# Two rounds of linear attention and feed-forward on one core: the attention's denominators spread by DMA instead of by matmuls, its sum over the rows cut in two halves, and the layer norms rearranged

## The chip, the cores and the metric

One core of a Trainium2 chip runs the whole program. The metric is the time of one execution in microseconds (us) of the device; the median of the runs shown is compared. A profiled execution, taken separately, gives the trace that every reading here comes from. Engines are named as the profile names them: PE (matrix multiply, with PEld for its weight loads), ACT (scalar engine), DVE (vector engine), POOL (GpSimd) and SP (the queue that issues DMAs).

## The reference

Two kinds of layer, each run twice on 2048 rows of 512 features (bf16), the second pair with the same weights as the first:

```
def _A_ref(x, wqkv, wo):                      # x: layer-normed rows
    H = 32; Dh = 16
    q, k, v = split(x @ wqkv)                 # 32 heads of 16
    phi = lambda t: where(t > 0, t + 1, exp(t)) + 1e-6
    pq, pk = phi(q), phi(k)
    kv  = einsum("bhsd,bhse->bhde", pk, v)    # sum over all rows
    z   = einsum("bhsd->bhd", pk)
    num = einsum("bhqd,bhde->bhqe", pq, kv)
    den = einsum("bhqd,bhd->bhq", pq, z)[..., None] + 1e-6
    return (num / den).reshape(B, S, D) @ wo

def _B_ref(x, w1, w2):                        # 512 -> 1376 -> 512
    return max(x @ w1, 0) @ w2

x = x + _A_ref(layernorm(x), wqkv, wo);  x = x + _B_ref(layernorm(x), w1, w2)
x = x + _A_ref(layernorm(x), wqkv, wo);  x = x + _B_ref(layernorm(x), w1, w2)
```

There is no mask and no position, so any order of the rows gives the same result as long as loads and stores agree.

## The kernel before

The 2048 rows are 16 tiles of 128 rows, and four tiles make a chunk (chunks 0 to 3). Layers 0 and 2 are attention, called A0 and A2 here; layers 1 and 3 are feed-forward, B1 and B3. All weights and activations stay in SBUF. `xn` holds the normed rows, `Tb` their transposes (features on partitions), `xres` the residual in f32.

An attention layer goes through these steps. `a_k` computes K of one tile (4 matmuls of 512 columns), `a_q` Q of one chunk, transposed (16 matmuls). `phi_evac` turns each into phi with two passes of ACT (lines 493 and 495) and two of DVE (497 and 503), into units of the buffer `big`. `a_z` sums phi(K) over the rows by matmuls of one column. `a_g` computes xn^T pk into four banks of PSUM (64 matmuls of 512 columns), from which `a_kv` makes K^T V by multiplying with the V weights, so that V itself is never computed. `a_m` masks the heads and multiplies by `wo`, giving `Mf` in four parts. `a_den` computes the denominators of a chunk, one row per head in a 32-row layout, and ACT takes their reciprocals as exp(-ln) into `rdc`. `a_pqs` spreads each reciprocal over the 16 rows of its head with four matmuls against the 0/1 matrix `Esel` (the group `rdc,Esel` of the profile) and multiplies phi(Q) by the result on DVE, out of PSUM (line 606). `a_fin` multiplies phi(Q) by `Mf` (16 matmuls per chunk), and `resid` adds it to the residual (DVE, line 521) and takes the sum of squares (ACT, line 527).

A feed-forward layer computes `h` per chunk in eleven parts, ten of 128 columns by `b_h` (40 matmuls) and one of 96 (`b_h_rest`, 16 matmuls of 96 columns, and a DMA transpose, line 642), and then `b_out`, eleven matmuls per tile.

Between two layers `ln_chunk` computes mean and variance of a chunk from the two sums in four small DVE steps (lines 439 to 445), a power of -1/2 on POOL (line 447) and one more DVE step (449). `ln_norm` then normalizes each tile on ACT, DVE or POOL. The transposes of a chunk go to the DMA (`transpose_chunk`, line 467) or, for the first chunk after an attention layer (`A_PE_CHUNKS=1`) and the first two chunks of the program (`FIRST_PE_CHUNKS=2`), to PE (`transpose_pe`, line 481) with an evacuation on ACT or DVE.

The order of instructions on each engine is fixed before the program runs. The code records every operation with its engine, what it reads and writes, and a planned duration, and `_list_schedule` goes through the records, giving PSUM banks (eight) and a place in an engine's order to whatever could start first within a window. Some operations may go to ACT or DVE, whichever would end first. Layers are interleaved: the steps of the next layer that need only finished chunks are put between the steps of this one. On the chip each engine then works through its list in order, waiting on semaphores; SP does the same with the DMAs. A step that waits therefore holds up everything behind it on its engine.

At the start `ld_x` loads x, in the order tile 0, the rest of chunk 0, K weights, Q weights, the other chunks, V weights, `wo`, `w1`, `w2`. Row 128n+p goes to partition p of tile n. The first DMA transpose waits for all loads (`ALL_LOADS`). While nothing has arrived, 16 matmuls on zeros run (`WARM`, line 399).

Of the kernel before, what the change touches and what calls it, by code (L numbers as in the profile page):

```python
# [16 lines left out]
C_MM128 = 58.0  # L17
C_MM96 = 43.0
# [14 lines left out]
C_POOL_POW = 1000.0  # L33
C_POOL_NORM = 900.0
C_SP_ISSUE = 60.0
TAIL = {PE: 70.0, ACT: 230.0, DVE: 80.0, POOL: 300.0, SP: 0.0}
# [208 lines left out]
def build_kernel(nc, A_x, A_wqkv, A_wo, B_w1, B_w2, out, n_layers_pairs=2, K_STT=0, Q_STT=0, A_PE_CHUNKS=1, windows=None,  # L245
                 WARM=16, SPLIT0=True, TAIL_SPLIT=True, LAST_HALVES=True, FIRST_PE_CHUNKS=2,
# [16 lines left out]
    UNITS = max(8, NFC) * NCH  # L263

    es = contextlib.ExitStack()
    with es:
# [14 lines left out]
        NL = 2  # L281
        lnd = sb("lnd", [128, NL, 512], F32)
        rdc = sb("rdc", [128, NCH, 512], BF16)
        hm128 = sb("hm128", [128, 4, 32], BF16)
        hm1 = sb("hm1", [128, 4, 32], F32)
        Esel = sb("Esel", [128, 128], BF16)
# [20 lines left out]
        veps0 = sb("veps0", [128, 1], F32)  # L307
        rstd0 = sb("rstd0", [128, 1], F32)
        nbias0 = sb("nbias0", [128, 1], F32)
# [28 lines left out]
        def dma(emit, reads, writes, xfer_ns, name):  # L338
            sem = es.enter_context(nc.semaphore("dsem%d" % len(dma_sems)))
            dma_sems.append(sem)  # L340

            def _emit(eng, emit=emit, sem=sem):
                return emit(eng).then_inc(sem, 16)
            op = g.add(SP, _emit, reads, writes, dur=C_SP_ISSUE, lat=xfer_ns, dma=True, name=name)
            op.seq = sem
            return op
# [17 lines left out]
        x_v = A_x[0].rearrange("(n p) d -> p n d", p=128)  # L364
        out_v = out[0].rearrange("(n p) d -> p n d", p=128)
        def ld_x(t, lo=0):
            dma(lambda e, t=t: e.dma_start(xin[:, 4 * t + lo:4 * t + 4, :], x_v[:, 4 * t + lo:4 * t + 4, :]),
                [], [("xin", i) for i in range(4 * t + lo, 4 * t + 4)], 1500.0 * (4 - lo) / 4.0, "ld_x%d" % t)
        dma(lambda e: e.dma_start(xin[:, 0, :], x_v[:, 0, :]), [], [("xin", 0)], 450.0, "ld_x0a")
        wq_v = A_wqkv.rearrange("(c p) n -> p c n", p=128)  # L370
        ld_x(0, 1)
        dma(lambda e: e.dma_start(wqkv[:, :, D:2 * D], wq_v[:, :, D:2 * D]), [], [("wk",)], 1500.0, "ld_wk")  # L372
        dma(lambda e: e.dma_start(wqkv[:, :, 0:D], wq_v[:, :, 0:D]), [], [("wq",)], 1500.0, "ld_wq")  # L373
        for t in range(1, NCH):
# [5 lines left out]
        dma(lambda e: e.dma_start(w1[:], B_w1.rearrange("(c p) n -> p c n", p=128)), [], [("w1",)], 4000.0, "ld_w1")  # L380
        dma(lambda e: e.dma_start(w2[:, 0:nfull, :], B_w2[0:nfull * 128, :].rearrange("(c p) n -> p c n", p=128)),
            [], [("w2a",)], 3800.0, "ld_w2a")
        if FLAST < 128:
            dma(lambda e: e.dma_start(w2[0:FLAST, NFC - 1, :], B_w2[nfull * 128:DFF, :]), [], [("w2b",)], 600.0, "ld_w2b")
        W2KEYS = [("w2a",), ("w2b",)] if FLAST < 128 else [("w2a",)]
        ALL_LOADS = [("wk",), ("wv",), ("wq",), ("wo",), ("w1",)] + W2KEYS
# [6 lines left out]
        if WARM > 0:  # L393
            wt = alloc_bank()

            def _warm(e):
                last = None
                for k in range(WARM):
                    last = e.matmul(psv[:, wt, :], wrm[:, 0:128], wrm[:, :], start=True, stop=True)
                return last  # L400
            g.add(PE, _warm, [("wrm",)], [("ps", wt)], WARM * 400.0, name="warm")
# [12 lines left out]
        ones_v = onesf[:, :].rearrange("p (j r) -> p j r", r=32)  # L414
        g.add(POOL, lambda e: e.affine_select(hm1[:], ones_v, [[0, 4], [-16, 32]], ALU.is_ge, 0.0, base=0, channel_multiplier=1),
              [("onesf",)], [("hm1",)], 350, name="as_h1")
        g.add(POOL, lambda e: e.affine_select(hm128[:], hm1[:], [[0, 4], [16, 32]], ALU.is_ge, 0.0, base=15, channel_multiplier=-1),
              [("hm1",)], [("hm128",)], 350, name="as_h2")

        def head_rows():  # L420
            b = alloc_bank()
            g.add(PE, lambda e: e.transpose(psv[:, b, 0:64].bitcast(BF16), hm128[:].rearrange("p j r -> p (j r)"), ident[:]),
                  [("hm128",), ("ident",)], [("ps", b)], C_MM128, name="trh")
            g.add(DVE, lambda e: e.tensor_copy(Esel[:], psv[:, b, 0:64].bitcast(BF16)), [("ps", b)], [("Esel",)], 200.0, name="esel")

        def ln_stats_first(i):
            g.add(DVE, lambda e: e.bn_stats(bst[:, i, :], xin[:, i, :]), [("xin", i)], [("bst", i)], C_DVE_BNST, name="bnst%d" % i)  # L427
            g.add(DVE, lambda e: e.bn_aggr(mv[:, i, :], bst[:, i, :]), [("bst", i)], [("mean", i), ("var", i)], C_DVE_SMALL, name="bnag%d" % i)

        def ln_chunk(t, first):  # L430
# [6 lines left out]
            else:  # L437
                mean_ap = mean[:, sl]
                g.add(DVE, lambda e: e.tensor_scalar(mean[:, sl], s1[:, sl], INV_D, None, ALU.mult),
                      [("s1", i) for i in tl], [("mean", i) for i in tl], C_DVE_SMALL, name="mean%d" % t)  # L440
                g.add(DVE, lambda e: e.scalar_tensor_tensor(nm2[:, sl], mean[:, sl], -1.0, mean[:, sl], ALU.mult, ALU.mult),
                      [("mean", i) for i in tl], [("nm2", t)], C_DVE_SMALL, name="nm2_%d" % t)
                g.add(DVE, lambda e: e.scalar_tensor_tensor(var[:, sl], s2[:, sl], INV_D, nm2[:, sl], ALU.mult, ALU.add),
                      [("s2", i) for i in tl] + [("nm2", t)], [("var", i) for i in tl], C_DVE_SMALL, name="var%d" % t)
                g.add(DVE, lambda e: e.tensor_scalar(veps[:, sl], var[:, sl], 0.0, EPS, ALU.max, ALU.add),  # L445
                      [("var", i) for i in tl], [("veps", t)], C_DVE_SMALL, name="veps%d" % t)
            g.add(POOL, lambda e: e.tensor_tensor(rstd[:, sl], veps[:, sl], nhalf[:, 0:4], ALU.pow),  # L447
                  [("veps", t), ("nhalf",)], [("rstd", t)], C_POOL_POW, name="rstd%d" % t)
            g.add(DVE, lambda e: e.scalar_tensor_tensor(nbias[:, sl], mean_ap, -1.0, rstd[:, sl], ALU.mult, ALU.mult),
                  [("mean", i) for i in tl] + [("rstd", t)], [("nbias", t)], C_DVE_SMALL, name="nbias%d" % t)  # L450

        def ln_norm(i, first):
            t = i // 4
            src = xin[:, i, :] if first else xres[:, i, :]
            skey = ("xin", i) if first else ("xres", i)
            rd = [skey, ("rstd", t), ("nbias", t)]
            alts = [(ACT, lambda e: e.activation(xn[:, i, :], src, ACTF.Identity, scale=rstd[:, i:i + 1], bias=nbias[:, i:i + 1]),
                     C_ACT_SB_AP),
                    (DVE, lambda e: e.tensor_scalar(xn[:, i, :], src, rstd[:, i:i + 1], nbias[:, i:i + 1], ALU.mult, ALU.add),  # L459
                     C_DVE_NORM_BF if first else 460.0)]  # L460
            if not first:
                alts.append((POOL, lambda e: e.tensor_scalar(xn[:, i, :], src, rstd[:, i:i + 1], nbias[:, i:i + 1], ALU.mult, ALU.add),
                             C_POOL_NORM))
            g.add_flex(alts, rd, [("xn", i)], name="norm%d" % i)

        def transpose_chunk(t, extra_reads=()):
            dma(lambda e: e.dma_start_transpose(Tb[:, 4 * t:4 * t + 4, :, :].rearrange("p i c t -> p (i c) t"),
                                                xn[:, 4 * t:4 * t + 4, :].rearrange("p i d -> p (i d)")),
                [("xn", i) for i in range(4 * t, 4 * t + 4)] + list(extra_reads),
                [("T", i) for i in range(4 * t, 4 * t + 4)], 2950.0, "tr%d" % t)  # L470
# [72 lines left out]
        def a_zc(ZB):  # L543
            g.add(DVE, lambda e: e.tensor_tensor(Zc[:], hm128[:], psv[:, ZB, 0:4].unsqueeze(2).broadcast_to([128, 4, 32]), ALU.mult),
                  [("ps", ZB), ("hm128",)], [("Zc",)], 200.0, name="zc")

        def a_g(m, i0, GB):
            def mk():
                mms = []
                for i in range(i0, i0 + 4):  # L550
                    u = pk_unit(i)
                    mms.append((psv[:, GB, :], xn[:, i, 128 * m:128 * m + 128], big[:, u * 512:u * 512 + 512],
                                i == 0, i == NT - 1, True))
                return mms
            mm_group(mk, [("xn", i) for i in range(i0, i0 + 4)] + [("big", pk_unit(i)) for i in range(i0, i0 + 4)],
                     [("ps", GB)], 4 * C_MM512, "g%d_%d" % (m, i0 // 4))

        def a_g_evac(m, GB):
            g.add_flex([(ACT, lambda e: e.activation(GT[:, m, :], psv[:, GB, :], ACTF.Identity), C_ACT_PSUM),
                        (DVE, lambda e: e.tensor_copy(GT[:, m, :], psv[:, GB, :]), C_DVE_FLEX)],  # L560
                       [("ps", GB)], [("GT", m)], name="gev%d" % m)

        def a_kv(m, KB):
# [410 lines left out]
```

## Time and profile before

| | us |
|---|---|
| median of 3 runs (293.8 to 294.86) | 294.8 |
| the profiled execution, as a run | 295.03 |
| its span in the trace | 293.3 |
| PE busy | 283.8 |
| ACT busy | 170.3 |
| DVE busy | 158.1 |
| POOL busy | 33.1 |

The span is measured from the first to the last instruction of the trace, so 1.7 us of the profiled run lie outside it. PE's ends are modelled, and a PE that is called busy may be waiting inside a group of matmuls; what a matmul really takes is read from the starts of one group after another. Sixteen matmuls of 512 columns take 3.45 us in this way (from 32.83 to 36.28 us of the trace), 0.216 us each, and the granted clock is 1.00 throughout.

### The profile page before, as it was taken

Reading aid. Unit: us, or ns where it says so; the run is one execution under the profiler, and the core shown is the slowest. Engines: PE = TensorE matmul, PEld = TensorE weight load, DVE = VectorE, ACT = ScalarE, POOL = GpSimd, SP = SyncE. Lnnn points to the kernel's source line nnn. Section 1 sums busy time; section 2 is a strip of 40 time slices with the busy share of each in tenths; the row PEclk is TensorE's granted clock in tenths of the full one; section 3 lists DMA queues with packets and bytes.
Section 4 is the critical chain, followed back from the end, with each engine's and each line's share of the span. In section 5 each row is a group of like instructions: output and inputs, shape, how many; then the busy total and the mean of one; then the engine's idle time right before and its main releaser. Section 6 shows DMA issues by size and latency. Waiting matters only on the chain.

```text
span 293.3 us, 4232 instructions
## 1 busy us (share of the span) xinstructions
PE 283.8 (97%) x1610; PEld 133.5 (46%) x1636; DVE 158.1 (54%) x443; ACT 170.3 (58%) x351; POOL 33.1 (11%) x43
## 2 busy tenths in 40 slices
PE   7699999989999999999999999999999999999996
PEld 3345444434454454454444444444445445454444
DVE  5699774999720293361454748928973037020122
ACT  2798496687765365397434999248786505407000
POOL 4012100002410040020020300000241002000000
PEclk9999999999999999999999999999999999999999
DMA  7991330000260016031003300000026003303022
GB/s 221 356 370 41 64 54 0 2 0 0 52 130 0 2 35 126 1 71 21 0 2 72 70 4 0 0 2 0 1 58 124 0 2 91 72 2 89 0 74 72
DMA packets 37796, 16.72 MB, mean 57 GB/s; under 512 B 29616, under 2 KB 37264, under 8 KB 37776
## 3 DMA queue, kind: packets, MB, share of 16 engines
q1 hardware_dynamic: 37776, 16.45, 22.8%
q8 instruction: 13, 0.21, 0.3%
q14 instruction: 7, 0.06, 0.1%
HBM read 7.01 MB, written 2.10 MB: 31 GB/s over the span
## 4 chain that ended last, share of the span: by engine, by line
PE 88%; DVE 6%; DMA 3%; ACT 2%; issue 1%; SPq 1%
PE ps L510 87%; DMA xin<-in_A_x_dram 3%; DVE big L606 2%; DVE xn L459 1%; DVE xres L521 1%; ACT Mf L576 1%; ACT big L493 1%; PE ps L481 0%; DVE bst L427 0%; DVE big L503 0%; DVE emscr L497 0%; ACT sqscr L527 0%; SPq L373 0%; ACT escr L495 0%; SPq L372 0%
## 5 line engine op out<-in xcount | busy, mean ns | idle before, releaser
L510 PE MATMUL ps<-w,big 128*128 128x512 bf16 (+3 forms) x355 | 76.0, 372 | 0.4
L510 PE MATMUL ps<-Tb,w 128*128 128x512 bf16 x320 | 70.4, 379 | 0.0
L510 PEld LDWEIGHTS ps<-w,big 128*128 128x128 bf16 (+1 forms) x363 | 35.3, 98 | 40.4
L527 ACT ACTIVATE sqscr<-xres 128x512 bf16<-128x512 f32 x48 | 30.0, 628 | 40.1 <-DVE xres L521 39.6
L655 ACT ACTIVATE big<-ps 128x512 bf16<-128x512 f32 x70 | 41.6, 598 | 17.9 <-PE ps L510 17.9
L510 PEld LDWEIGHTS ps<-Tb,w 128*128 128x128 bf16 x320 | 30.8, 98 | 35.9
L493 ACT ACTIVATE big<-ps 128x512 bf16<-128x512 f32 x64 | 41.2, 648 | 9.0 <-PE ps L510 8.8
L521 DVE SCALAR_TENSOR_TENSOR xres<-ps,xres 128x512 f32<-128x512 f32 x32 | 21.9, 689 | 38.2 <-PE ps L510 38.0
L495 ACT ACTIVATE escr<-ps 128x512 bf16<-128x512 f32 x64 | 41.6, 667 | 0.4 <-DVE emscr L497 0.4
L447 POOL TENSOR_TENSOR rstd<-veps,nhalf 128x4 f32<-128x4 f32 x15 | 16.1, 1070 | 204.5 <-DVE veps L445 183.3
L518 DVE TENSOR_TENSOR xin<-ps,xres 128x512 bf16<-128x512 f32 x15 | 10.4, 692 | 46.6 <-PE ps L510 46.6
L510 PE MATMUL ps<-wqkv,Tb 128*128 128x512 bf16 x122 | 28.6, 379 | 2.7 <-DVE Tb L486 1.2
L510 PE MATMUL ps<-Tb,wqkv 128*128 128x512 bf16 x128 | 30.6, 379 | 0.0
L510 PE MATMUL ps<-Mf,big 128*128 128x512 bf16 x122 | 29.0, 380 | 1.3 <-ACT Mf L576 0.8
L510 PE MATMUL ps<-big,xn 128*128 128x512 bf16 x124 | 29.7, 379 | 0.3
L497 DVE TENSOR_SCALAR emscr<-escr 128x512 bf16<-128x512 bf16 x64 | 18.4, 296 | 18.5 <-ACT escr L495 18.4
L503 DVE TENSOR_TENSOR big<-big,emscr 128x512 bf16<-128x512 bf16 x64 | 26.4, 421 | 1.2
L606 DVE TENSOR_TENSOR big<-big,ps 128x512 bf16<-128x512 bf16 x32 | 19.9, 680 | 1.3 <-PE ps L510 1.3
L510 PEld LDWEIGHTS ps<-wqkv,Tb 128*128 128x128 bf16 x128 | 12.1, 98 | 17.2 <-DVE Tb L486 1.7
L510 PEld LDWEIGHTS ps<-Mf,big 128*128 128x128 bf16 x128 | 11.9, 98 | 16.2 <-ACT Mf L576 1.3
L510 PEld LDWEIGHTS ps<-big,xn 128*128 128x128 bf16 x128 | 11.5, 97 | 13.1 <-issue 1.5
L510 PEld LDWEIGHTS ps<-Tb,wqkv 128*128 128x128 bf16 x128 | 11.5, 97 | 12.3 <-DVE big L606 0.4
(74 smaller groups left out, 196.2 us busy)
## 6 DMA issues: line engine op xcount, KB each, us to landing
wqkv<-in_A_wqkv_dram SPq DMA_DIRECT2D x3, 512.0 KB, 7.1
xin<-in_A_x_dram SPq DMA_DIRECT2D x3, 512.0 KB, 9.1
out_dram<-xin SPq DMA_DIRECT2D x3, 512.0 KB, 2.9
w<-in_B_w_dram SPq DMA_DIRECT2D x1, 1376.0 KB, 11.0
w<-in_B_w_dram SPq DMA_DIRECT2D x1, 1280.0 KB, 12.8
wo<-in_A_wo_dram SPq DMA_DIRECT2D x1, 512.0 KB, 9.4
xin<-in_A_x_dram SPq DMA_DIRECT2D x1, 384.0 KB, 3.2
out_dram<-xin SPq DMA_DIRECT2D x1, 256.0 KB, 2.1
```

The lines of the kernel that those rows point to most:

```text
L447: g.add(POOL, lambda e: e.tensor_tensor(rstd[:, sl], veps[:, sl], nhalf[:, 0:4], ALU.pow), [("veps", t), ("nhalf",)], [("rstd", t)], C_POO ...
L459: (DVE, lambda e: e.tensor_scalar(xn[:, i, :], src, rstd[:, i:i + 1], nbias[:, i:i + 1], ALU.mult, ALU.add), C_DVE_NORM_BF if first else 4 ...
L493: g.add(ACT, lambda e: e.activation(dst_ap, psv[:, b, :], ACTF.Identity, bias=1.0 + 1e-6, scale=1.0), [("ps", b)], [dst_key], C_ACT_PSUM, ...
L495: g.add(ACT, lambda e: e.activation(escr[:, s, :], psv[:, b, :], ACTF.Exp), [("ps", b)], [("escr", s)], C_ACT_EXP, name=name + "_exp")
L497: g.add(DVE, lambda e: e.tensor_scalar(emscr[:, s, :], escr[:, s, :], 1.0, 1e-6, ALU.min, ALU.add), [("escr", s)], [("emscr", s)], C_DVE_B ...
L503: g.add(DVE, lambda e: e.tensor_tensor(dst_ap, dst_ap, emscr[:, s, :], ALU.max), [dst_key, ("emscr", s)], [dst_key], 340.0, name=name + "_ ...
L510: last = e.matmul(o, l, r, start=st, stop=sp, skip_group_check=skip)
L518: g.add(DVE, lambda e: e.tensor_tensor(xin[:, i, :], psv[:, b, :], src, ALU.add), [("ps", b), skey], [("xin", i)], C_DVE_PSUM, name="resid ...
L521: g.add(DVE, lambda e: e.scalar_tensor_tensor(xres[:, i, :], psv[:, b, :], 0.0, src, ALU.add, ALU.add, accum_out=s1[:, i:i + 1]), [("ps", ...
L527: g.add(ACT, lambda e: e.activation(sqscr[:, q, :], xres[:, i, :], ACTF.Square, accum_out=s2[:, i:i + 1]), [("xres", i)], [("sqscr", q), ( ...
L606: g.add(DVE, lambda e, j=j, u=u: e.tensor_tensor(unit_ap(u), unit_ap(u), psv[:, bs[j], :], ALU.mult), [("ps", bs[j]), ("big", u)], [("big" ...
L655: g.add_flex([(ACT, lambda e, M=M, b=b, u=u: e.activation(unit_ap(u, M), psv[0:M, b, :], ACTF.Relu), C_ACT_PSUM), (DVE, lambda e, M=M, b=b ...
```

## The change

- Denominators. `a_pqs` has no matmuls any more. The reciprocals `rdc` are copied by four DMAs from SBUF to SBUF (`a_spread`), each source row to four partitions, into units of `big`, and DVE multiplies two SBUF tiles. For this each row of `a_den`'s result now stands for a head four times (`hm32` in place of `hm128` and `Esel`). Chunk 0 is spread by itself, chunks 1 and 2 together, chunk 3 by itself.
- xn^T pk. `a_g` works on 256 of the 512 columns. The first half is computed chunk by chunk while K and Q are, in both attention layers; the second half in `bar`. `a_kv`, `a_m` and the evacuations are done per half. `a_fin` of the first six tiles is split into j = 0, 1 and j = 2, 3, so that the first part needs only the first half.
- Norms between layers. The small steps of `ln_chunk` move from DVE to POOL, five of them before the power and one behind it. DVE and POOL normalize with (x + (-mean)) * rstd; each tile of a chunk has a fixed engine (two DVE, one ACT, one POOL).
- Transposes. `A_PE_CHUNKS` is 0: the first chunk after an attention layer is transposed by two DMAs of two tiles. The first DMA transpose no longer waits for `w1` and `w2`; these are loaded after the transposes of chunks 2 and 3 have landed.
- Start. Tiles 0 to 3 have a chain each (`ln_own`): statistics, power, normalization, PE transposes. Tile 3's statistics are taken on ACT. Partition p holds rows 16p to 16p+15, so a load or store of several tiles is contiguous for each partition. 13 warming matmuls.
- The planner's durations are adjusted (for example POOL's tail of 300 ns becomes 60, the issue of a DMA transpose 1200), which shifts the order on every engine.

```
-    A_PE_CHUNKS=1, WARM=16
+    A_PE_CHUNKS=0, WARM=13
+        FIN_SPLIT = 6
-        x_v = A_x[0].rearrange("(n p) d -> p n d", p=128)
+        x_v = A_x[0].rearrange("(p n) d -> p n d", p=128)
+        def ld_ff():
+            after = [("T", i) for i in range(4 * FIRST_PE_CHUNKS, NT)]
+            dma(..., after, [("w1",)], 4000.0, "ld_w1")
...
-        ALL_LOADS = [("wk",), ("wv",), ("wq",), ("wo",), ("w1",)] + W2KEYS
+        ALL_LOADS = [("wk",), ("wv",), ("wq",), ("wo",)]
...
         def ln_chunk(t, first):
-                g.add(DVE, lambda e: e.tensor_scalar(mean[:, sl], s1[:, sl], INV_D, None, ALU.mult), ...
-                g.add(DVE, lambda e: e.scalar_tensor_tensor(nm2[:, sl], mean[:, sl], -1.0, mean[:, sl], ALU.mult, ALU.mult), ...
-                g.add(DVE, lambda e: e.scalar_tensor_tensor(var[:, sl], s2[:, sl], INV_D, nm2[:, sl], ALU.mult, ALU.add), ...
-                g.add(DVE, lambda e: e.tensor_scalar(veps[:, sl], var[:, sl], 0.0, EPS, ALU.max, ALU.add), ...
+                g.add(POOL, lambda e: e.tensor_scalar(mean[:, sl], s1[:, sl], -INV_D, None, ALU.mult), ...
+                g.add(POOL, lambda e: e.tensor_tensor(nm2[:, sl], s1[:, sl], mean[:, sl], ALU.mult), ...
+                g.add(POOL, lambda e: e.tensor_scalar(nm2[:, sl], nm2[:, sl], D * EPS, None, ALU.add), ...
+                g.add(POOL, lambda e: e.tensor_tensor(var[:, sl], s2[:, sl], nm2[:, sl], ALU.add), ...
+                g.add(POOL, lambda e: e.tensor_scalar(veps[:, sl], var[:, sl], INV_D, EPS, ALU.mult, ALU.max), ...
             g.add(POOL, lambda e: e.tensor_tensor(rstd[:, sl], veps[:, sl], nhalf[:, 0:4], ALU.pow), ...
...
+        def a_g(m, i0, n, hf, GB, col, opens):
...
+                    mms.append((psv[:, GB, col:col + 256], xn[:, i, 128 * m:128 * m + 128],
+                                big[:, u * 512 + 256 * hf:u * 512 + 256 * hf + 256], opens and i == 0, i == NT - 1, True))
...
+        def a_spread(t0, n):
+            w = 512 * n
+            for j in range(4):
+                u = rb_unit(t0, j)
+                dma(lambda e, j=j, u=u: e.dma_start(big[:, u * 512:u * 512 + w],
+                                                    rdc[32 * j:32 * j + 32, t0:t0 + n, :].rearrange("p t q -> p (t q)")
+                                                    .unsqueeze(1).broadcast_to([32, 4, w])), ...
         def a_pqs(t):
-            bs = [alloc_bank() for _ in range(4)]
-            mm_group(lambda: [(psv[:, bs[j], :], Esel[32 * j:32 * j + 32, :], rdc[32 * j:32 * j + 32, t, :], ...
             for j in range(4):
-                g.add(DVE, lambda e, j=j, u=u: e.tensor_tensor(unit_ap(u), unit_ap(u), psv[:, bs[j], :], ALU.mult), ...
+                u, r = pq_unit(j, t), rb_unit(t, j)
+                g.add(DVE, lambda e, u=u, r=r: e.tensor_tensor(unit_ap(u), unit_ap(u), unit_ap(r), ALU.mult), ...
...
+        def a_fin_chunk(t, first_layer):
+            if t == 0:
+                for i in range(FIN_SPLIT):
+                    fin_open[i] = alloc_bank()
+                    a_fin_mm(i, fin_open[i], (0, 1))
...
+        def ln_own(i):
+            g.add(POOL, lambda e: e.tensor_tensor(rstd[:, i:i + 1], veps[:, i:i + 1], nhalf[:, 0:1], ALU.pow), ...
+            g.add(DVE, lambda e: e.tensor_scalar(xn[:, i, :], xin[:, i, :], mu, rstd[:, i:i + 1], ALU.subtract, ALU.mult), ...
+            transpose_pe(i)
...
                 def bar():
+                    g_a(NCH - 1)
...
+                    a_den(NCH - 1)
+                    a_spread(NCH - 1, 1)
...
                 def p2(t):
-                    for i in range(4 * t, 4 * t + 4):
-                        a_fin(i, first_layer)
-                    ln_next(t, t < A_PE_CHUNKS)
+                    a_fin_chunk(t, first_layer)
...
+                    ln_next(t, t < A_PE_CHUNKS, 2 if t == 0 else 1)
```

In the order that the planner makes of this, all 64 matmuls of `a_fin` of a layer now stand together (before, twelve of them stood behind the first feed-forward chunks), and DVE's list holds the multiplications by spread reciprocals between other steps: in A0 the phi of Q's last tile behind the second DMA of chunk 0, and the first residual of chunk 0 behind the first DMA of chunk 3; in A2 the second half's head mask behind the third DMA of chunk 3.

## The prediction

> **What bounds the kernel now.** I read the page's busy times and chain of waits first, then PE's instructions in order of time, then the ends of the waits in the first 35 us and between A0 and B1.
>
> ```profile
> PE 283.8 (97%) x1610; PEld 133.5 (46%) x1636; DVE 158.1 (54%) x443; ACT 170.3 (58%) x351; POOL 33.1 (11%) x43
> PE 88%; DVE 6%; DMA 3%; ACT 2%; issue 1%; SPq 1%
> ```
>
> PE is the bound nearly everywhere, so a change pays where it takes matmuls off PE or closes one of PE's few gaps, and costs where it opens one. In PE's order of time (start, length, line, group, idle before):
>
> ```profile
> 17.01 1.36 PE L481 MATMUL ps<-ident,xn 128*128 128x128 bf16 x16
> 19.29 3.40 PE L510 MATMUL ps<-wqkv,Tb 128*128 128x512 bf16 x15
> 32.83 3.62 PE L510 MATMUL ps<-wqkv,Tb 128*128 128x512 bf16 x16
> 50.26 1.03 PE L510 MATMUL ps<-big,xn 128*128 128x512 bf16 x4
> 51.22 0.39 PE L510 MATMUL ps<-rdc,Esel 32*128 32x512 bf16 x4
> 51.55 0.40 PE L510 MATMUL ps<-GT,wqkv 128*128 128x128 bf16 x4
> ...
> 60.22 3.63 PE L510 MATMUL ps<-Mf,big 128*128 128x512 bf16 x16 [0.79 <-ACT Mf L576]
> ...
> 67.14 3.63 PE L510 MATMUL ps<-Mf,big 128*128 128x512 bf16 x15
> 70.60 1.06 PE L481 MATMUL ps<-ident,xn 128*128 128x128 bf16 x16
> 71.75 1.90 PE L510 MATMUL ps<-Mf,big 128*128 128x512 bf16 x8
> 73.49 0.84 PE L510 MATMUL ps<-w,Tb 128*128 128x96 bf16 x16
> ...
> 166.03 0.25 PE L510 MATMUL ps<-ones,big 128*128 128x1 bf16 x4 [0.41 <-DVE big L503]
> ```
>
> The reader should subtract starts, not add lengths: a length holds 0.16 us of pipeline that overlaps the next group. Four xn^T pk matmuls from 50.26 end their turn at 50.26 + 4 x 0.216 = 51.12; the next group but one starts at 51.55, so the spreading group takes 0.43.
>
> For what replaces PE's work, the DMAs to landing and POOL's power:
>
> ```profile
> Tb<-xn SPq DMA_TRANSPOSE x12, 4.3
> xin<-in_A_x_dram SPq DMA_DIRECT2D x1, 128.0 KB, 2.2
> big<-hr SPq DMA_TRANSPOSE x8, 2.4
> out_dram<-xin SPq DMA_DIRECT2D x1, 128.0 KB, 1.7
> ```
>
> ```profile
> 23.57 1.65 POOL L447 TENSOR_TENSOR rstd<-veps,nhalf 128x4 f32<-128x4 f32 x1 [7.35 <-DVE veps L435]
> 66.91 1.01 POOL L447 TENSOR_TENSOR rstd<-veps,nhalf 128x4 f32<-128x4 f32 x1 [33.82 <-DVE veps L445]
> ```
>
> **The parts, one by one.** The sum is against the profiled execution: span 293.3, run 295.03, 0.2 above the median of 294.8. What comes off the span I take off the median.
>
> *Spreading matmuls.* Eight groups (four chunks, two layers) of 0.43: **-3.4**. Their DVE multiply (line 606, eight in 4.87 us, 0.61 each out of PSUM) becomes an SBUF one like line 503 (two in 0.75 us), 32 x 0.24 = 7.7 us of DVE, worth nothing on PE by itself. In exchange twelve DMAs per layer go to SP. The trace has no SBUF-to-SBUF copy. Nearest rows of 128 KB: 1.7 and 2.2; farthest that fits a DMA inside the core, 4.3 for a transpose. I take 2.2 (same size, same kind of instruction), and 0.6 for issuing one (rows 0.40 to 0.51 on SP). SP has nothing else queued: in A0 `w1`, `w2` are issued ahead of them once chunk 3's transpose has landed (issued at 34.7 as before, plus 4.5), from about 39 to 47 (before, they landed 7.3 us after `wo`; B1 needs them at 72), and the first reciprocal is ready at about 50; the first transpose behind them is needed at 67. Walking A0 by these: chunk 0's second copy lands at 53.0, Q's last phi behind it on DVE is done at 53.7, `a_den` of chunk 3 reads it at 54.5; chunk 3's first copy lands at 60.1, the first residual behind it could start at 60.7. A2's third copy of chunk 3 lands 0.4 before the mask behind it is due. All covered, by half a microsecond each.
>
> *PE transposes between layers.* 67.14 + 16 x 0.216 = 70.60 to 71.75 is 1.15 with its 0.28 idle; twice: **-2.3**. Now the DMA path must be ready when the 64 `a_fin` matmuls end, since the 96-column group behind them needs all of chunk 0, and all of the feed-forward layer stands behind that group on PE. A0: first residual 60.7; DVE does four (0.69 each), three multiplies (0.34), three more residuals, then two norms (0.55 each), to 67.7. Meanwhile ACT's squares (0.7 each) and POOL run beside it. SP issues two half transposes. One of 4 blocks lands after 2.4 and one of 16 after 4.3, so 8 blocks about 3.0; the second is issued 1.4 behind the first: 67.75 + 4.5 = 72.3. PE would end `a_fin` at 71.4: wait 0.9. A2: with F the first `a_fin`, its first tile ends at F + 3.7, DVE has nine residuals ahead of the norms, which end at F + 11.1; landing at F + 15.6; PE is through at F + 14.4: wait 1.3 with the start. Together **+2.1**; bounds 0 (landing of 4.3 for both at once and norms sooner) and 4.3.
>
> *Small steps on POOL.* Not in the trace; between a 128x4 memset (0.10) and the power (1.01). The power's own rows (0.56, 0.86, 1.01 for 1, 3, 4 columns) leave 0.41 at no column, so I take 0.2, below it. Behind the last square stand two steps and the power; at 0.2, and at 0.41 too, the result arrives before DVE has finished the residuals that are ahead of its norms (slack 0.7 and 1.05): **0**. At 1.01 seven steps in a row make A0's last normalization end 3 us later. The rows also show POOL slowed to 1.65 beside DVE's two-input bf16 work at 23.57; the residuals read PSUM, and 66.91 beside them is 1.01.
>
> The Trainium skill ("GPSIMD Engine Reference", "Performance versus the Vector engine") speaks against this: ordinary elementwise work belongs on the vector engine, about twice as fast. The trace has no such pair of this size; by the rule, DVE's rows of 0.16 would become 0.32, which is still inside the slack, and the sum would stay.
>
> It also ("VectorE: DVE Perf Modes", "Rules for kernel authors") prefers TensorE for a 128x128 transpose, giving 1309 ns for the DMA against 390. The trace has sixteen in 4.3 us by DMA, not 21, and 1.15 us of PE's own time by matmul; by the page's figure the wait would be some 16 us longer twice and the change a heavy loss.
>
> *xn^T pk in halves.* 256 matmuls of 256 columns for 128 of 512. At the end of the trace, eleven of 256 columns separate two DVE steps:
>
> ```profile
> 289.50 0.42 DVE L674 TENSOR_TENSOR xin<-ps,xres 128x256 bf16<-128x256 f32 x1 [0.51 <-PE ps L510]
> 290.71 0.42 DVE L674 TENSOR_TENSOR xin<-ps,xres 128x256 bf16<-128x256 f32 x1 [0.78 <-PE ps L510]
> ```
>
> 1.21 / 11 = 0.110; 256 x 0.110 - 128 x 0.216 = **+0.5**. What it buys: `Mf` of the first half is ready while the second is summed, and the idle ahead of 60.22 goes (60.22 less 59.25, where the four Q matmuls from 58.39 end: 0.97), as does 0.41 at 166.03, where more matmuls now fill. I charge 0.4 for a new wait in A0 (the denominators' weights follow the last column sums by 0.96 before, with 0.44 of work between now) and 0.2 for the second half's `Mf`: **-0.8**.
>
> *Start.* x of chunk 1 landed at 10.9; the 0.5 MB loads behind it land 1.5 apart. Longer rows gain 0 to 1.5 of that; I take 0.3. The norms of chunk 1 then start at 16.4 (before 16.54), as DVE is the limit there. PE by then has one Q group, the column sums and eight half sums more behind it, and K of chunk 1 starts at 18.2 against 19.1. Then 12.55 us of work leads to K of chunk 2 at 30.75. Its transpose is issued when DVE is through, 26.6, and lands 4.5 later: 31.1 against 32.83, same matmuls done: **-1.7** (bounds -0.6, if chunk 1 lands no sooner and DVE's order loses, and -2.3). Fewer warming matmuls are hidden by the wait for tile 0.
>
> *Feed-forward* is as before: **0**, as PE is dense there and its transposes have microseconds to spare (chunk 1 lands at 77.5, needed at 81.7); the tail too.
>
> Sum: -3.4 - 2.3 + 2.1 + 0.5 - 0.8 - 1.7 = -5.6; 294.8 - 5.6 = **289.2**.
>
> **The rivals.** *The new waits are fully covered* (faster still): halves land together, the start gives 2.3 and the 0.6 of small waits falls away: 289.2 - 2.1 - 0.6 - 0.6 = 285.9. For: 0.9 and 1.3 are small against chains of ten steps. Against: DVE's residuals alone take 11 us beside 14 of `a_fin`.
>
> *The copies take 4.3* as a transpose does. Then A0's last phi is 1.6 late for PE and the first residual another 1.7: 3.3; A2's mask and `Mf` 1.4. 289.2 + 4.7 = 293.9. Against: rows of 1.7 and 2.2.
>
> *Slower: the copies queue*, landing 7.1 after issue as the 512 KB weight loads do. Place: DVE's order in `bar`. Price: 4.9 later than assumed, counted twice in A0 (first in Q's last phi, again in chunk 3's reciprocals, which follow from it) less 0.9 of slack, 8.9, and 4.4 in A2: 289.2 + 13.3 = 302.5. It decides from a landing of 4.6, where the 5.6 is used up. For: four at once on one queue, and 0.5 us of slack. Against: the weight loads had up to 2 MB ahead of them, these have 128 to 256 KB.
>
> *POOL's small steps cost what the power does*, 1.01: 2.3 in A0, 3.0 in A2, 0.8 where B1 hands chunk 3 to A2: 295.3, no change. Against: a memset of the same shape takes 0.10.
>
> **Chances.** Forecast 0.57 (own range 287 to 291.5), fully covered 0.18, copies at 4.3 0.10, copies queue 0.08, slow POOL 0.07. Range 285.6 to 293.8: the two next cases are in, the slower two are out, 0.15, with a little beyond the low end. A difference under 0.5% (1.5 us) can't be told from none: faster means below 293.3. Of the copies at 4.3 0.06 is there, of slow POOL 0.03: faster 0.57 + 0.18 + 0.06 + 0.03 = 0.84, same 0.08, slower 0.08.
>
> **What would show it.** No `rdc,Esel` group and PE busy some 5 less; copies landing in 2.2 (below 4.6); idle of PE of about 1 ahead of the first 96-column group of B1 and B3, ended by a DMA; K of chunk 2 at about 31; POOL's small steps near 0.2. The forecast is wrong if PE idles inside `bar`, or by over 2 ahead of those two groups.

## The result, and the profile after

The changed kernel takes 291.64 us in the median of four executions (291.34 to 291.85), beside 294.3 for the kernel before in the same set (293.73 to 294.86): a ratio of 0.9908, with a 95% interval from 0.989 to 0.9926. (The 294.8 of the prediction is the median of three of these four.) It is faster by 2.7 us, as forecast in direction and inside the range, but by half of the 5.6 that the terms add up to. The profiled executions differ by 3.4 (span 293.3 before, 289.9 after); the one of before, 295.03 as a run, is slower than all four, so 0.7 of the 3.4 belongs to that execution.

Two lines of the page of the changed kernel (busy times; the chain of waits), and the answer on what TensorE (PE) waited for (the engine, its tile and line, what ended the wait, then us in total, times, longest):

```profile
PE 280.1 (97%) x1696; PEld 143.4 (49%) x1696; DVE 139.6 (48%) x379; ACT 170.3 (59%) x352; POOL 53.2 (18%) x119
PE 71%; DVE 11%; DMA 8%; ACT 4%; POOL 2%; SPq 1%; issue 1%; POOLq 0%
```

```profile
PE ps L523 <- DMA Tb<-xn: 2.4, 3, 1.1
PE ps L523 <- DVE big L516: 1.6, 2, 1.0
...
PE ps L494 <- DVE xn L760: 0.8, 1, 0.8
PE ps L523 <- DVE KVT L590: 0.7, 2, 0.5
```

PE has 3.7 less to do, but the last work to end now runs through other engines and DMAs for 29% of the span, where it was 12%. PE's instructions in order of time at the places where the two kernels part (start, length, group, idle before):

```profile
18.49 3.62 PE L523 MATMUL ps<-wqkv,Tb 128*128 128x512 bf16 x16
...
31.86 1.90 PE L523 MATMUL ps<-wqkv,Tb 128*128 128x512 bf16 x8 [0.66 <-DMA Tb<-xn]
34.08 2.02 PE L523 MATMUL ps<-wqkv,Tb 128*128 128x512 bf16 x8 [0.31 <-ACT escr L508]
...
36.29 1.04 PE L523 MATMUL ps<-Tb,wqkv 128*128 128x512 bf16 x4
...
56.21 0.40 PE L523 MATMUL ps<-big,Zc 128*32 128x512 bf16 x4 [0.60 <-DVE big L516]
...
61.17 0.60 PE L523 MATMUL ps<-wo,KVT 128*128 128x512 bf16 x2 [0.52 <-DVE KVT L590]
61.61 12.35 PE L523 MATMUL ps<-Mf,big 128*128 128x512 bf16 x56
75.09 0.85 PE L523 MATMUL ps<-w,Tb 128*128 128x96 bf16 x16 [1.14 <-DMA Tb<-xn]
...
211.75 0.85 PE L523 MATMUL ps<-w,Tb 128*128 128x96 bf16 x16 [0.63 <-DMA Tb<-xn]
```

The second 96-column group of this kind in the kernel before:

```profile
212.58 0.84 PE L510 MATMUL ps<-w,Tb 128*128 128x96 bf16 x16
```

These groups divide the run. Before, the first stood at 73.49 with 12 of the 64 `a_fin` matmuls still behind it, so the same work was done by 73.49 + 12 x 0.216 = 76.08; now at 75.09, where all 64 are done. By the second it is 212.58 + 2.59 = 215.17 against 211.75. From there to the end it is 78.1 in both. So the start and A0 gave 0.99, B1 and A2 2.43, B3 nothing. By the prediction's terms it was 3.9 and 1.7: A2 did better than forecast, and the whole shortfall, 2.9, lies ahead of 75.09.

What DVE did in A0's bar, and what the DMAs and POOL took (the page's DMA issues: number, size, median us to landing; then POOL's instructions at the start, and the two steps of DVE that wait for them):

```profile
54.21 0.43 DVE L637 TENSOR_TENSOR big<-big 128x512 bf16<-128x512 bf16 x1 [0.30 <-DMA big<-rdc]
...
55.40 0.43 DVE L637 TENSOR_TENSOR big<-big 128x512 bf16<-128x512 bf16 x1 [0.22 <-DMA big<-rdc]
55.74 0.42 DVE L516 TENSOR_TENSOR big<-big,emscr 128x512 bf16<-128x512 bf16 x1
...
60.01 0.76 DVE L637 TENSOR_TENSOR big<-big 128x512 bf16<-128x512 bf16 x2 [0.81 <-DMA big<-rdc]
60.69 0.42 DVE L590 TENSOR_TENSOR KVT<-ps,bmask 128x256 bf16<-128x256 f32 x1
...
62.48 1.10 DVE L637 TENSOR_TENSOR big<-big 128x512 bf16<-128x512 bf16 x3
63.49 0.69 DVE L534 SCALAR_TENSOR_TENSOR xres<-ps,xin 128x512 f32<-128x512 f32 x1
...
68.96 1.00 DVE L473 TENSOR_SCALAR xn<-xres,mean,rstd 128x512 bf16<-128x512 f32 x2
```

```profile
big<-rdc SPq DMA_DIRECT2D x16, 128.0 KB, 2.7
big<-rdc SPq DMA_DIRECT2D x8, 256.0 KB, 4.7
```

```profile
13.96 2.06 POOL L448 TENSOR_TENSOR rstd<-veps,nhalf 128x4 f32<-128x4 f32 x1 [5.26 <-DVE veps L435]
23.38 2.19 POOL L448 TENSOR_TENSOR rstd<-veps,nhalf 128x4 f32<-128x4 f32 x1 [7.35 <-DVE veps L435]
```

```profile
16.06 0.16 DVE L451 SCALAR_TENSOR_TENSOR nbias<-mv,rstd 128x4 f32<-128x4 f32 x1 [0.91 <-POOL rstd L448]
...
25.60 0.16 DVE L451 SCALAR_TENSOR_TENSOR nbias<-mv,rstd 128x4 f32<-128x4 f32 x1 [0.90 <-POOL rstd L448]
```

The reader sees two things that the prediction had smaller. The multiplies (L637) wait for copies, and behind them in DVE's fixed order stand Q's last phi (L516), the second half's mask (L590) and the first residual (L534), at 63.49 where 60.7 was forecast; PE's 0.60 and 0.52 are its waits for the first two. And the power at the start takes 2.06 and 2.19, where the kernel before had 1.31 and 1.65; DVE waits 0.9 for each.

### The profile page after: what moved, and what is told of

The parts are those of the page before. It is cut to its first block, busy times and chain, and to the rows that moved or that the text cites. A ratio compares the mean times of both kernels' runs of the same rounds, so it can differ in the third digit from the quotient of the medians.

```text
span 289.9 us, 4431 instructions
## 1 busy us (share of the span) xinstructions
PE 280.1 (97%) x1696; PEld 143.4 (49%) x1696; DVE 139.6 (48%) x379; ACT 170.3 (59%) x352; POOL 53.2 (18%) x119
## 4 chain that ended last, share of the span: by engine, by line
PE 71%; DVE 11%; DMA 8%; ACT 4%; POOL 2%; SPq 1%; issue 1%; POOLq 0%
PE ps L523 71%; DMA Tb<-xn 4%; DVE xres L534 3%; DMA big<-rdc 3%; DVE bst L427 2%; POOL rstd L448 2%; ACT big L506 2%; DMA xin<-in_A_x_dram 1%; SPq L628 1%; ACT escr L508 1%; DVE big L637 1%; DVE xn L463 1%; ACT lnd L616 1%; DVE xn L473 1%; DVE big L516 1%
## 5 line engine op out<-in xcount | busy, mean ns | idle before, releaser
L523 PE MATMUL ps<-w,big 128*128 128x512 bf16 (+2 forms) x363 | 77.3, 372 | 0.0
L700 ACT ACTIVATE big<-ps 128x512 bf16<-128x512 f32 x74 | 44.1, 597 | 18.0 <-PE ps L523 17.9
L506 ACT ACTIVATE big<-ps 128x512 bf16<-128x512 f32 x64 | 40.0, 626 | 9.6 <-PE ps L523 9.2
L534 DVE SCALAR_TENSOR_TENSOR xres<-ps,xres 128x512 f32<-128x512 f32 x32 | 21.1, 687 | 43.5 <-PE ps L523 43.5
L508 ACT ACTIVATE escr<-ps 128x512 bf16<-128x512 f32 x64 | 40.5, 633 | 0.0
L523 PE MATMUL ps<-big,xn 128*128 128x256 bf16 x256 | 31.8, 272 | 0.0
L523 PE MATMUL ps<-wqkv,Tb 128*128 128x512 bf16 x128 | 29.7, 379 | 1.0 <-DMA Tb<-xn 0.7
L523 PE MATMUL ps<-Tb,wqkv 128*128 128x512 bf16 x128 | 29.8, 379 | 0.1
L438 POOL TENSOR_SCALAR mean<-s 128x4 f32<-128x4 f32 x12 | 2.9, 239 | 136.8 <-DVE xres L534 136.8
L516 DVE TENSOR_TENSOR big<-big,emscr 128x512 bf16<-128x512 bf16 x64 | 26.9, 426 | 1.3
L523 PEld LDWEIGHTS ps<-big,xn 128*128 128x128 bf16 x256 | 23.8, 98 | 4.4 <-issue 0.9
L448 POOL TENSOR_TENSOR rstd<-veps,nhalf 128x4 f32<-128x4 f32 x15 | 17.7, 1177 | 20.6 <-DVE veps L435 19.6
```

The source lines that it names most:

```text
L438: g.add(POOL, lambda e: e.tensor_scalar(mean[:, sl], s1[:, sl], -INV_D, None, ALU.mult), [("s1", i) for i in tl], [("mean", i) for i in tl ...
L506: g.add(ACT, lambda e: e.activation(dst_ap, psv[:, b, :], ACTF.Identity, bias=1.0 + 1e-6, scale=1.0), [("ps", b)], [dst_key], C_ACT_PSUM, ...
L508: g.add(ACT, lambda e: e.activation(escr[:, s, :], psv[:, b, :], ACTF.Exp), [("ps", b)], [("escr", s)], C_ACT_EXP, name=name + "_exp")
L516: g.add(DVE, lambda e: e.tensor_tensor(dst_ap, dst_ap, emscr[:, s, :], ALU.max), [dst_key, ("emscr", s)], [dst_key], 340.0, name=name + "_ ...
L523: last = e.matmul(o, l, r, start=st, stop=sp, skip_group_check=skip)
L534: g.add(DVE, lambda e: e.scalar_tensor_tensor(xres[:, i, :], psv[:, b, :], 0.0, src, ALU.add, ALU.add, accum_out=s1[:, i:i + 1]), [("ps", ...
```

## The experiments

All are against the kernel before, five rounds each, on the chip; the changed kernel's 291.64 is the other mark.

**1. Spreading on PE again, in the changed kernel.** In place of `a_spread`, one matmul per column group against a 0.25-weighted selection:

```diff
-  e.tensor_tensor(unit_ap(u), unit_ap(u), unit_ap(r), ALU.mult)
+  mm_group([(psv[:, b, :], Esel[32*j:32*j+32, :], rdc[32*j:32*j+32, t, :], True, True, False)])
+  e.tensor_tensor(unit_ap(u), unit_ap(u), psv[:, b, :], ALU.mult)
```

> The changed kernel with the denominators spread by TensorE again (one 32-row matmul per column group against a 0.25-weighted selection, DVE multiplies out of PSUM) in place of the SBUF copies. My theory (matmuls cost PE 8 x 0.43 = 3.4 us, and the copies give back only the waits that the trace shows behind them, 0.60 + 0.52 + 0.20 = 1.3): 291.6 + 3.4 - 1.3 = 293.7, PE busy up by about 3, no wait of DVE for a DMA of the reciprocals. Rival (the copies give the whole gain back in A0's bar by late landings): 290.5 to 291.6, with A2 slower and A0 faster than with copies.

Measured 299.14, ratio 1.0182 (1.015 to 1.0214), PE busy 287.2. Both theories missed. Three of the six executions, 299.8 to 301.4, had a granted clock of 0.989 to 0.993; the profiled one, 298.48, had 1.00 and is still 6.8 above the changed kernel. PE's order in A0 shows why:

```profile
59.08 0.79 PE L525 MATMUL ps<-rdc,Esel 32*128 32x512 bf16 x2
60.08 0.38 PE L525 MATMUL ps<-rdc,Esel 32*128 32x512 bf16 x1 [0.21 <-DVE big L641]
...
61.50 0.98 PE L525 MATMUL ps<-rdc,Esel 32*128 32x512 bf16 x3
62.41 4.49 PE L525 MATMUL ps<-Mf,big 128*128 128x512 bf16 x20
```

In this order of steps the groups come late and one by one, and PE goes at the pace of DVE's multiplies out of PSUM (0.68 each), which must free a bank first. This run prices an order, not the term; the seventh does that.

**2. Chunk 0 transposed by PE again, in the changed kernel:** `A_PE_CHUNKS=1`.

> The changed kernel with chunk 0 transposed by TensorE again between attention and feed-forward, nothing else. My theory (transposes cost PE 2 x 0.9 and the waits of 1.14 and 0.63 ahead of the two 96-column groups go): 291.6 + 1.8 - 1.8 = 291.6, a swap, no more than 0.5 either way. Rival (the waits are set by the late residuals and normalizations, and only change their name): 291.6 + 1.8 = 293.4, with idle of PE left ahead of the two groups. Rival (the DMA transposes cost more than their waits show): 290.5 or less.

Measured 291.59, ratio 0.9911 (0.9899 to 0.9923): the swap of my theory. In the changed kernel this part gives nothing.

**3. Small norm steps on DVE again, in the changed kernel** (five steps and the bias; `g.add(POOL, ...)` to `g.add(DVE, ...)`).

> The changed kernel with the small norm steps between the layers on DVE again, the power left on GpSimd. My theory (behind the last square only two steps of 0.3 stand, DVE would do them in 2 x 0.16 but behind a residual of 0.61): 291.6, within 0.5; PE's waits for the transposes of chunk 0 stay at 1.1 and 0.6 within 0.4. Rival (GpSimd's pitch of 0.3 for each of seven steps sets the transposes' issue): both waits shrink by about 1, 290.0 to 290.6.

Measured 298.69, ratio 1.0153 (1.0133 to 1.0172): 7 slower than the changed kernel, against both. DVE in A0, then PE in order of time, then windows in A0 and A2 (us; PE's busy time and instructions; granted clock; DMA share; GB/s):

```profile
67.26 0.15 DVE L440 TENSOR_TENSOR nm<-s,mean 128x4 f32<-128x4 f32 x1
67.33 0.68 DVE L534 SCALAR_TENSOR_TENSOR xres<-ps,xin 128x512 f32<-128x512 f32 x1
...
67.94 0.16 DVE L442 TENSOR_SCALAR nm<-nm 128x4 f32<-128x4 f32 x1
```

```profile
76.84 1.46 PE L523 MATMUL ps<-w,Tb 128*128 128x96 bf16 x16 [3.18 <-DMA Tb<-xn]
78.10 11.05 PE L523 MATMUL ps<-Tb,w 128*128 128x512 bf16 x40
```

```profile
74.00:77.00 3.00, 0.16 (x3) 0.81 0.95 135
77.00:80.00 3.00, 3.00 (x21) 0.50 0.74 94
80.00:84.00 4.00, 4.00 (x14) 0.67 0.45 98
84.00:88.00 4.00, 4.00 (x20) 1.00 0.70 131
...
216.00:220.00 4.00, 2.12 (x21) 0.90 0.65 125
220.00:224.00 4.00, 4.00 (x14) 0.67 1.16 178
```

Each step stands behind one more residual, 0.68 a step where POOL has a pitch of 0.3, so `veps` ends 1.7 later (69.47 against 67.81) and PE waits 3.18 instead of 1.14 (2.40 instead of 0.63 in A2), 3.8 more. After the wait the granted clock is 0.50, and the 40 matmuls take 10.9 instead of 8.6 (from the start of the group to the start of the next), the 96-column group 0.6 more, and in A2 the 40 take 10.3: 4.5 more. Together 8.3, less 0.3 by which `a_fin` of A0 came sooner; the span grew by 7.8. So more than half of the 7 is the clock that the longer waits cost, and the rest the waits.

**4. The copies planned as measured, in the changed kernel.** Only the planner's durations change, and with them DVE's order:

```diff
-  650.0 if n == 1 else 1250.0, "spread%d_%d" % (t0, j), issue=620.0)
+  900.0 if n == 1 else 1500.0, "spread%d_%d" % (t0, j), issue=700.0 if n == 1 else 1100.0)
```

> The changed kernel with the planner's times of the spreading copies nearer to what the trace shows (900 and 1500 ns a transfer in place of 650 and 1250, 700 and 1100 ns an issue in place of 620): the same instructions, DVE's order put together anew, the first mask and the first residuals ahead of the multiplies of chunks 1 and 2. My theory (the loss in A0 is DVE's fixed order behind copies that land late): the 0.52 ahead of the second half's mask, about 0.4 hidden behind its evacuation and some 0.5 of the wait for chunk 0's transposes go: 290.2, 289.8 to 290.9. Rival (the copies' landing itself is what PE waits for, in whatever order): 291.6, waits of the same sum elsewhere.

Measured 290.89, ratio 0.9888 (0.9874 to 0.9902): 0.75 better than the changed kernel, at the edge of my theory and not the rival's. The 0.52 for the mask went, the 0.60 for Q's last phi, and A2's 0.63; A0's wait for the transposes stayed, 1.09, since PE came earlier too, and two new waits of DVE's work opened inside `a_fin`, so that less than half of the 1.75 was kept:

```profile
63.76 9.67 PE L523 MATMUL ps<-Mf,big 128*128 128x512 bf16 x43 [0.45 <-DVE big L637]
...
199.38 11.40 PE L523 MATMUL ps<-Mf,big 128*128 128x512 bf16 x51 [0.35 <-DVE Mf L598]
```

**5 and 6. One and two parts alone, on the kernel before:** `A_PE_CHUNKS=0`; the same with the small steps on POOL, the normalizations on fixed engines and POOL's planned tail of 60.

> The kernel before with one part of the change alone: chunk 0 transposed by DMA between attention and feed-forward, the small norm steps still on DVE. My theory after the third experiment (each small step on DVE stands behind a residual, so the transposes land some 3 late, and an idle of 3 on TensorE is followed by some 2 at a lower clock, twice): 294.3 - 2.3 + 2 x 3.2 + 2 x 2 = 302.4, at least 298. Rival (the prediction's sum taken term by term, -2.3 + 2.1, with the small steps worth nothing): 294.1.

> The kernel before with two parts: chunk 0 transposed by DMA, and the small norm steps on GpSimd with the normalizations shared out as in the changed kernel. My theory (the two parts pay only together: waits of 1.1 and 0.6 in place of 2 x 1.15): 294.3 - 2.3 + 1.8 = 293.8, 293.0 to 295.0, and at least 4 below the run with the first part alone. Rival (GpSimd's steps help only where the residuals come out of half sums, as in the changed kernel): as the run with the first part alone, 298 or more.

Measured 292.53 (ratio 0.994, 0.9924 to 0.9957) and 293.23 (0.9964, 0.995 to 0.9977). My theory fell: DMA transposes alone gain 1.65, small steps on DVE and all. In the fifth run (PE, and DVE's first residual and first norms):

```profile
74.81 0.85 PE L510 MATMUL ps<-w,Tb 128*128 128x96 bf16 x16 [0.20 <-DMA Tb<-xn]
```

```profile
60.90 0.68 DVE L521 SCALAR_TENSOR_TENSOR xres<-ps,xin 128x512 f32<-128x512 f32 x1
...
68.93 1.09 DVE L459 TENSOR_SCALAR xn<-xres,rstd,nbias 128x512 bf16<-128x512 f32 x2
```

Whole output tiles end 0.87 apart there, which leaves DVE room for the small steps between residuals of 0.61, and the first residual is at 60.90. In the changed kernel it is at 63.49, six tiles are begun with half of `Mf`, their other halves end 0.43 apart, and DVE is never free until the norms. So the small steps cost only there. Whether the late start or the half tiles pack the residuals these runs don't separate. The sixth run's 0.7 goes with a wait of 1.18 for ScalarE in A2's K that the fifth doesn't have; I put it down to the new order, which no run tries by itself.

**7. The copies alone, on the kernel before** (`a_spread` and the new head mask in place of `Esel`).

> The kernel before with one part alone: the denominators spread by the SBUF copies, in the same twelve DMAs per attention layer, DVE's multiplies out of SBUF. My theory (-3.4 of matmuls as the prediction put it, +1.3 of waits as in the changed kernel): 292.2, 291.3 to 293.0, PE busy down by about 3. Rival (the copies are given back by their landing): 294.0 or more.

Measured 292.16, ratio 0.9926 (0.9911 to 0.9942), PE busy 280.3: in size as my theory had it, though its waits are not those of the changed kernel (0.70 ahead of chunk 3's denominators, 0.44 and 0.34 inside the transposes). Copies landed in 2.7 and 4.7 here too.

**8. The start's powers on ScalarE, in the changed kernel:**

```diff
-  POOL: tensor_tensor(rstd[:, sl], veps[:, sl], nhalf[:, 0:4], ALU.pow)
+  ACT: activation(nm2[:, sl], veps[:, sl], Ln); activation(rstd[:, sl], nm2[:, sl], Exp, scale=-0.5)
```

> The changed kernel with the inverse roots of chunks 1 to 3 at the start computed on ScalarE (ln, then exp of minus a half) in place of GpSimd's power, which took 2.1 there beside DVE. My theory (DVE's two waits of 0.9 for it delay chunk 1's column sums and chunk 2's transpose, and PE's waits of 0.98, 0.66 and 0.3 come from there): K of chunk 2 starts at about 31.0 instead of 31.9, 290.6, 290.0 to 291.0. Rival (DVE's own queue is the limit at the start, the waits move): 291.6 within 0.4. Rival (ScalarE's evacuations ahead of the two steps make them as late): 291.6 or more.

Measured 290.09, ratio 0.986 (0.9838 to 0.9882): 1.55 better than the changed kernel, which neither rival allows. K of chunk 2 in its trace, beside 31.86 and 34.08:

```profile
31.04 1.67 PE L528 MATMUL ps<-wqkv,Tb 128*128 128x512 bf16 x7 [0.59 <-DMA Tb<-xn]
33.02 2.02 PE L528 MATMUL ps<-wqkv,Tb 128*128 128x512 bf16 x8 [0.31 <-ACT escr L513]
```

**9, 10 and 11. Whole sums instead of halves, and the two cures together.** The ninth takes xn^T pk, mask, `Mf`, `a_fin` and attention's order of steps from the kernel before, the rest from the changed one; the tenth adds the edits of runs 8 and 4; the eleventh is the changed kernel with these two.

> The changed kernel with one part undone: xn^T pk summed in whole columns again, the mask, Mf and the output matmuls in one piece, attention's steps in the order of the kernel before, with the copies, the DMA transposes, the small steps and the start of the changed kernel. My theory (the six output tiles that are begun with half of Mf push the first residual back by 6 x 0.43, and the residuals then come closer together than DVE does them, so the transposes of chunk 0 are late; alone on the kernel before, the copies gave 2.1 and the DMA transposes 1.7, and the start gave 1.2 in the changed one): 294.2 - 2.1 - 1.7 - 1.2 = 289.2, 288.5 to 290.4, idle ahead of the two 96-column groups under 0.4. Rival (the prediction's terms for the halves, +0.5 and -0.8, hold and undoing them costs): 291.9 or more, with 0.8 ahead of the first output matmul in A0.

> The ninth experiment's kernel with two further edits that gained in the changed one: the start's inverse roots on ScalarE (1.5) and the copies planned later (0.7). My theory: the first is in the start and adds up, the second was a cure for multiplies ahead of the second mask, which is gone here: 289.2 - 1.5 = 287.7, 287.0 to 288.9. Rival (the start's gain is lost before A0 ends, since DVE holds the bar): as the ninth.

> The changed kernel with the start's inverse roots on ScalarE and the copies planned later, halves kept. My theory: the two act at different places and add up, 291.6 - 1.5 - 0.7 = 289.4, 288.9 to 289.9. Rival (earlier starts only lengthen the wait for chunk 0's transposes): 290.0 or more.

The ninth: median 294.11, ratio 0.9979 (0.9957 to 1.0002). Its twelve executions follow the granted clock: four at 1.000 took 292.0 to 292.5, six at 0.993 to 0.994 took 293.3 to 294.4, two at 0.988 took 295.0 and 295.5. The profiled one is among the first:

```profile
71.84 1.90 PE L522 MATMUL ps<-Mf,big 128*128 128x512 bf16 x8 [3.50 <-DVE big L629]
73.58 0.84 PE L522 MATMUL ps<-w,Tb 128*128 128x96 bf16 x16
```

As I expected there is no idle ahead of the 96-column group; but the time didn't come, not even at 1.000. The order of before has chunk 3's Q last, so its reciprocals, its copies (issued from 66.19) and its multiplies end at 71.78, and PE waits 3.50 for them. Part of this is DVE's order: the multiplies stand behind chunk 0's norms and start at 69.91 without a wait for a copy. In the fifth run, with matmuls, that path was covered; here it isn't. The tenth, median 291.88 (0.9897, 0.9875 to 0.9919), shows the same wait, 0.82 in A0 and 2.34 in A2; its executions are 290.3 at a clock of 0.999 and 291.8 to 292.2 at 0.993 to 0.994. Both forecasts missed, and these two runs move Q and the norms along with the halves, so they don't price the halves.

The eleventh: 289.39, ratio 0.9831 (0.9818 to 0.9843). The two cures add up (1.55 + 0.75 of 291.64 is 289.34).

**12. Four multiplies on POOL, in the eleventh's kernel:** `a_pqs(2, POOL, 1200.0)` in A0.

> The eleventh experiment's kernel with the four multiplies of chunk 2 in the first attention layer on GpSimd, which is idle there until the small norm steps at about 64.6. My theory (in A0's bar DVE is the engine that is late: its multiplies of 0.34 stand between the evacuation of Mf and the residuals, and PE's wait of 1.09 for chunk 0's transposes follows from them): four multiplies less are 1.4 of DVE, some 0.7 of them ahead of chunk 0's last residual, 289.4 - 0.7 = 288.7, 288.3 to 289.1. Rival (GpSimd is held up beside DVE's two-input bf16 work, as its power at the start was, 2 or more for each multiply): they end past 66, where the output matmuls of chunk 2 and the small steps behind them need GpSimd, 290 or more.

Measured 288.85 (288.69 to 289.38), ratio 0.9817 (0.979 to 0.9844). POOL, DVE and PE in its bar:

```profile
58.77 3.80 POOL L642 TENSOR_TENSOR big<-big 128x512 bf16<-128x512 bf16 x3 [0.24 <-DMA big<-rdc]
```

```profile
62.02 0.83 DVE L642 TENSOR_TENSOR big<-big 128x512 bf16<-128x512 bf16 x1
```

```profile
62.91 9.67 PE L528 MATMUL ps<-Mf,big 128*128 128x512 bf16 x43 [0.85 <-DVE big L642]
72.78 0.85 PE L528 MATMUL ps<-w,Tb 128*128 128x96 bf16 x16 [0.20 <-DMA Tb<-xn]
```

The same two places in the eleventh:

```profile
62.22 9.67 PE L528 MATMUL ps<-Mf,big 128*128 128x512 bf16 x44 [0.45 <-DVE big L642]
72.98 0.85 PE L528 MATMUL ps<-w,Tb 128*128 128x96 bf16 x16 [1.09 <-DMA Tb<-xn]
```

The wait for the transposes fell from 1.09 to 0.20, but mostly because PE came 0.7 later: a multiply of chunk 1 that DVE still has took 0.83 beside POOL's, and PE's wait for it grew from 0.45 to 0.85. The group behind the transposes starts only 0.2 sooner, and the first residual came no sooner (60.80 against 60.51), so the path is not the one I gave. The median is the lowest of all, 5.5 under the kernel before, and lies in the forecast; but the executions overlap with the eleventh's (289.25 to 289.81) and the two profiled ones differ by 0.2, so a gain over the eleventh is not shown.

## Why the prediction was right, and where its sizes were off

*The sign and the main terms.* Both rows of matmuls were on PE's path, as the prediction put it: alone on the kernel before, the copies gave 2.0 (run 7) and the DMA transposes 1.65 (run 5), beside terms of -3.4 and of -2.3 with a wait. PE's busy time fell by 3.5 in run 7 (283.8 to 280.3), near the 3.4 of the copies' term; some 1.4 of it came back as waits.

*Waits after `a_fin`.* Forecast 0.9 and 1.3, measured 1.14 and 0.63: near in sum, with some luck. In A0 both sides of the forecast's difference were late by about as much, PE through at 73.95 (75.09 less 1.14) instead of 71.4 and the landing at 75.09 instead of 72.3. The transposes as such don't make the wait: in run 5 the norms of chunk 0 start at 68.93 and PE's wait ends at 74.81, in the changed kernel at 68.96 and 75.09, with PE there 0.7 sooner. PE's work got shorter, DVE's chain up to chunk 0's norms did not; how much of that is the half tiles and how much the late copies stays open.

*Small steps on POOL.* Taken at 0.2, measured 0.20 to 0.34 at a pitch of 0.3. The prediction's 0 says only that they add nothing where POOL has them. That leaving them on DVE would cost 7 (run 3) it didn't see, since it never walked that case.

*Start, -1.7.* Mis-sized. K of chunk 2 came at 31.86, not 31.1; counting half sums done earlier that is 0.97 + 0.27 = 1.24. K's second half then lost some 0.5 at 34.08, and Q of chunk 2 starts at 36.29, beside 36.28 before, so about 0.4 of work done earlier is what is left there. The step that failed is taking DVE as the limit and the power at about its old length: the denser DVE work held POOL's power to 2.06 and 2.19, DVE then stood idle 0.9 for each, and the transpose was issued at 27.42, not 26.6. Run 8, without these powers, put K at 31.04 and paid 1.55.

*"All covered, by half a microsecond each".* This is the other failing step. Copies of 128 KB took 2.7 (3.2 to 3.5 for the first in A0) and those of 256 KB 4.7, where 2.2 was taken for all, and the first was issued at 50.97, not 50; the margins were 0.5. PE idled inside `bar`, 0.60 and 0.52 where 0.4 was charged, which the prediction had named as the sign against it. Run 4, which only let DVE pass the late copies by, paid 0.75.

*The sum.* Of the 2.9 that is missing ahead of 75.09, the start is some 1.3, the waits inside `bar` 0.7 and the wait for the transposes 0.2; 0.7 has no place yet. A2's wait was 0.63 instead of 1.3, which is most of what it did better. With both failing steps mended, run 11 takes 289.39 beside 294.42 for the kernel before in its set, 5.0 of the 5.6; that the figure is so near 289.2 is in part chance, as the terms differ one by one. The time of 291.64 lies just outside the forecast's own 287 to 291.5: the wide range held because it took in most of the way to the rival of slow copies (293.9, landing in 4.3), and the 256 KB copies did take 4.7. What remains unsettled is the halves by themselves: runs 9 and 10 undo them, but move chunk 3's Q too, so +0.5 and -0.8 were not tried apart.

## What to carry to other kernels

When a transfer replaces an engine's work, put its landing time, once measured, into whatever fixes the order: here the engine that waited for copies also held a mask and a residual that could go sooner, and 0.75 us came back by the order alone, without changing an instruction. Price a part by putting it alone on the old kernel and by taking it out of the new one, and expect the two to differ: the transposes were worth 1.65 and 0, the small steps no gain and 7. Look at the absolute times as well as at a wait: in run 12 a wait of 1.09 shrank to 0.20 and only 0.2 us was won. Leave no cover of half a microsecond unexamined in a chain of ten steps.

## What the runs showed of the hardware

A POOL instruction and DVE's bf16 steps in SBUF can hold each other up. The 128x4 power took 1.01 to 1.04 beside residuals out of PSUM; beside the phi's bf16 steps it took 1.31 and 1.65 in the kernel before and 2.06 and 2.19 in the changed one, and each of these four ended 0.86 to 0.88 after the last of the back-to-back bf16 steps that DVE had begun with. In run 12 a DVE multiply that started while POOL's last multiply ran took 0.83 instead of 0.42; three that started just ahead of one of POOL's (57.09 against 57.14) kept their 0.42. The Trainium skill ("SBUF — State Buffer", "SBUF: two separate sides") says that the two engines share a pair of ports as an exclusive lock, held for a whole instruction by whichever starts first. These rows agree that the first comes first and the other waits. One row doesn't fit the whole instruction: in run 12 a DVE multiply at 66.22 took 0.42 inside a power of POOL's from 65.88 to 66.92, which took 1.04.

PE's granted clock was 0.50 for a while around the long waits of run 3. By stretches of one us, all of which have 1.00 or 0.50 but for the ends, it was low for 6.8 us in A0, from 75.8, inside an idle of 3.18, to 82.7, and for 3.4 in A2, from 219.2, 1.3 after work had resumed behind an idle of 2.40, to 222.6: two pieces of 3.4 and one. In run 9 an idle of 3.50 left the clock at 1.00 in the profiled execution, while others of the same kernel had means of 0.994 and 0.988, which over their 293 us is some 3.5 and 7 us at 0.50. So the length of the idle alone doesn't decide. The Trainium skill ("TensorE: Matmul & The Clock Gate", "What's actually happening") gives a free-running window of about 3.4 us, and the pieces of 3.4 and the differences between executions of one kernel fit that.
